# Grouped-query attention with a cached K and V: the last batches' order of work, a second buffer for turned probabilities, batch 31 placed by VectorE and ScalarE, and its V fetched in two loads

## The chip, the cores and the metric

The kernel runs on one core of one Trainium2 chip. A core has five engines that run their own instruction lists and wait for one another by semaphores: TensorE (PE, matrix products; its weight loads appear as PEld), VectorE (DVE), ScalarE (ACT), GpSimd (POOL) and SyncE (SP, which here only issues DMA transfers). The metric is the device time of one execution in microseconds, as the median of several runs; lower is better.

## The reference

For 32 batches of 4 new tokens, queries are projected, attend over a cache of 2048 keys and values in 4 KV heads (each shared by 8 of the 32 query heads), and the result is projected back:

```
B, Sq, D = 32, 4, 1024;  Hq, Hkv, Sk, Dh = 32, 4, 2048, 128
q = (x @ wq) as [B, Hq, Sq, Dh]
scores = einsum(q, k) * Dh ** -0.5          # k, v: the KV head of query head h is h // 8
p = softmax(scores)
o = einsum(p, v)                            # [B, Hq, Sq, Dh]
out = o as [B, Sq, Hq * Dh] @ wo
```

All arrays are bf16. The K and V caches are 2 MB for each batch and each of the two, 128 MB in all; wq and wo are 8 MB each.

## The kernel before

Everything is written in raw engine instructions. A small class, `Program`, keeps one ordered list of operations for each engine; an operation names the events that it waits for, and events of an engine become counts of that engine's semaphore. So **the order of the lists is the schedule**: each engine takes its own list strictly in order, and whatever stands behind a waiting operation waits too.

**Loads.** SP issues one stream: wq in 4 loads, then K and V of the batches in turn, then wo, all through a ring of 7 slots of 16 KB per partition (`slots`, `stream`, lines 145 to 186). A load waits until the operation that frees its slot is done (`freed`): the last transposition of a K (`("kt", b, 7)`) or the last quarter of a V's product (`("pv", b, 3)`). The first wo slot takes that of V of batch 26, the next that of K of 31, then V of 27, then V of 28. wo comes in ten loads (seven of 1 MB, then 512, 256 and 256 KB), each with its own semaphore.

**One batch b** passes these steps, with 128 rows = 4 KV heads x 32 (8 query heads x 4 tokens):

1. `kt_fill(b, f)`, f = 0 to 7 (PE, line 245): 8 transpositions each of K into one of three PSUM banks `ps_a`, `ps_b`, `ps_c` in turn; `evac` copies the bank to `KT_sb` (L379 on DVE, L381 on ACT; ACT takes fills 0, 1 and 7, DVE the others).
2. `qk(b, c)` (PE, line 257): the scores, 16 matmuls into `ps_s`, which holds one batch. It waits for the exponential of the batch before (`exp`), which reads `ps_s`.
3. `dve_max` (L436, L437): row maximum of the scores and its scaled negative; `act_exp` (L495): the exponential of `ps_s` into `P_sb` with the row sums. It also waits for the turn of the batch before, which reads `P_sb`.
4. `dve_turn` (L441, L442): reciprocal of the sums, and P turned in blocks of 32 x 32 from `P_sb` into `PC_sb`. `PC_sb` is one buffer: the turn waits until all four placements of the batch before have read it.
5. `place(eng, b, g)`, g = 0 to 3: rows 32g to 32g+31 of `PC_sb` go to their block of `PD_sb` (two buffers, by b modulo 2; L397 on ACT, L399 on POOL or DVE). The table `PLACE` says which engine: POOL takes three and ACT one; for batches 29 and 30 POOL takes g 0 and 1, DVE g 2, ACT g 3; for batch 31 POOL takes g 0, DVE g 1 and 2, ACT g 3.
6. `pv(b, quarter)` (PE, line 276): P times V, 16 matmuls a quarter. It waits for V's load and all four placements.
7. `dve_o` (L453) scales the product by the reciprocal sums into `o_sb`; `o_tr` (PE, line 303, called "ot" in PE's list) transposes it; `dve_ot` (L448) copies that to `oT_sb`.

At the end `oproj` (PE, line 355) multiplies `oT_sb` by wo: 64 matmuls of 512 columns in `ps_s`, in the order of the ten wo loads, two column halves for each row block. It waits for every `ot`. Then DVE (L487) copies the left half of the result and ACT (L515) the right half to `out_sb` (which is `PC_sb`), both when the last matmul is done, and SP stores it.

In the main loop (batches 0 to 28) PE's list runs the scores of batch i, the transpositions of K of i+2 and the product with V of i-2 in alternation. **The tail** is a list written out by hand. PE's list at lines 341 to 348 has: scores of 29, six fills of K of 31, the whole product of 27, scores of 30, the last two fills, ot of 27, the product of 28, scores of 31, and then the products of 29, 30 and 31, each with the ot of the batch before set in after its first quarter (for 31 after its third). DVE's list (lines 466 to 487) and ACT's (lines 507 to 515) are written to match: DVE has turn of 29, o of 27, max of 30, fill 6, ot of 27, its place of 29, o of 28, turn of 30, max of 31, ot of 28, its place of 30, o of 29, turn of 31, ot of 29, two places of 31, o and ot of 30, o and ot of 31. ACT has exp of 29, its place of 29, fill 7, exp of 30, its place of 30, exp of 31, its place of 31.

Of the kernel before, what the change touches and what calls it, by code (L numbers as in the profile page):

```python
# [5 lines left out]
ACT = mybir.ActivationFunctionType  # L6
# [49 lines left out]
def bass_standalone__gqa_block_cached__sampling_kernel(  # L56
# [28 lines left out]
    PLACE = {b: ("pool", "pool", "pool", "act") for b in range(B)}  # L85
    for b in (B - 3, B - 2):
        PLACE[b] = ("pool", "pool", "dve", "act")
    PLACE[B - 1] = ("pool", "dve", "dve", "act")
    QUARTERS = 4
    WQ_LOADS = 4  # L90
    WO_LOADS = 4
    WE = 4
# [9 lines left out]
    with ExitStack() as es:  # L102
# [3 lines left out]
        QT_sb = sb("QT_sb", [128, B, Hq, Sq], BF16)  # L106
        oT_sb = sb("oT_sb", [128, WE, WO_BLOCKS, NT], BF16)
        P_all = sb("P_sb", [128, Sk], BF16)
        PC_all = sb("PC_sb", [128, NJ // 2, 64], BF16)
        PD_sb = sb("PD_sb", [128, 2, NJ // 2, 128, 2], BF16)  # L110
        o_sb = sb("o_sb", [128, WE, Dh], BF16)
        mask = sb("mask", [128, WE], BF16)
# [4 lines left out]
        ssum = sb("ssum", [128, B], F32)  # L117
        rinv = sb("rinv", [128, B], F32)
        P_sb = P_all[:, :]
        PC_sb = PC_all[:, :, :]  # L120
        PC_flat = PC_sb.rearrange("p a b -> p (a b)")
        x_sb = P_all[:, 0:D]
        xT_sb = P_all[:, D:2 * D].rearrange("p (a b) -> p a b", b=128)
        out_sb = PC_flat[:, 0:D]

        ps_s = es.enter_context(nc.psum_tensor("ps_s", [128, Sk], F32))
        ring = [es.enter_context(nc.psum_tensor(f"ps_{c}", [128, 512], F32)) for c in "abco"]
# [12 lines left out]
        q_bank = ring_f32 + [ps_s[:, c * 512:(c + 1) * 512] for c in range(4)]  # L140

        pr.sems = {e: es.enter_context(nc.semaphore(f"s_{e}")) for e in Program.ENGINES}
        for n in ["x", "out"] + [f"slot{i}" for i in range(NSLOT)] + [f"wo{i}" for i in range(sum(map(len, WO_CUTS)))]:
            pr.sems[n] = es.enter_context(nc.semaphore(f"s_{n}"))


# [13 lines left out]
        def slot(l):  # L160
            return slots[:, slot_of[l], :]
# [4 lines left out]
        def fetch(dst, src):  # L166
            return lambda e: e.dma_start(dst, src)
# [3 lines left out]
        for n, l in enumerate(stream):  # L171
            kind, i = l
            waits = [freed(stream[n - NSLOT])] if n >= NSLOT else []
            s, v = f"slot{n % NSLOT}", 16 * (n // NSLOT + 1)
            if kind == "wq":
                pr.load("sp", fetch(slot(l), wq_v[:, i, :]), l, s, v, waits)
            elif kind in "kv":
                src = (k_cache if kind == "k" else v_cache)[i].rearrange("g (p t) d -> (g p) (t d)", t=NJ)
                pr.load("sp", fetch(slot(l), src), l, s, v, waits)
            else:  # L180
                for k in range(i * BPL, (i + 1) * BPL):
                    for e0, e1 in WO_CUTS[k]:
                        at = (k - i * BPL) * WE * D
                        part = slot(l)[:, at + e0 * D:at + e1 * D]
                        pr.load("sp", fetch(part, wo_v[k][:, e0 * D:e1 * D]), ("wo", k, e0), f"wo{n_wo}", 16, waits)
                        n_wo += 1
# [4 lines left out]
        jobs = [("kt", b, f) for b in range(B) for f in range(FILLS)]  # L191
        job_index = {j: n for n, j in enumerate(jobs)}

        def consumer(f):
            return "act" if f in ACT_FILLS else "dve"

        def ring_waits(job):
            n = job_index[job]
# [73 lines left out]
        def pv(b, quarter):  # L272
            def fn(e):
                v = slot(("v", b))
                for j in range(quarter * NJ // QUARTERS, (quarter + 1) * NJ // QUARTERS):
                    ins = e.matmul(  # L276
                        o_bank(b),
                        lhsT=PD_sb[:, b % 2, j // 2, :, j % 2],
                        rhs=v[:, j * Dh:(j + 1) * Dh],
                        start=(j == 0),  # L280
                        stop=(j == NJ - 1),
                    )
                return ins

            w = [("v", b)] + [("place", b, g) for g in range(G)]
            if b == 0:
                w += [("q_evac", 3)]
            elif b <= DRAIN - 2:
                w += [("o", b - 1), ("ot", b - 1)]
            elif b == DRAIN - 1:  # L290
                w += [("evac",) + last_in(1)]
            else:
                w += [("o", b - 2), ("ot", DRAIN - 2)]
            pr.op("pe", fn, w, ("pv", b, quarter))
# [35 lines left out]
        for i in range(DRAIN):  # L330
# [9 lines left out]
            pe_run(steps)  # L340
        pe_run([
            ("qk", B - 3, ()), ("kt", B - 1, (0, 1, 2, 3, 4, 5)),
            ("pv", B - 5, (0, 1, 2, 3)), ("qk", B - 2, ()), ("kt", B - 1, (6, 7)), ("ot", B - 5, ()),
            ("pv", B - 4, (0, 1, 2, 3)), ("qk", B - 1, ()),
            ("pv", B - 3, (0,)), ("ot", B - 4, ()), ("pv", B - 3, (1, 2, 3)),
            ("pv", B - 2, (0,)), ("ot", B - 3, ()), ("pv", B - 2, (1, 2, 3)),
            ("pv", B - 1, (0, 1, 2)), ("ot", B - 2, ()), ("pv", B - 1, (3,)), ("ot", B - 1, ()),
        ])

        def oproj(k, e0, e1):  # L350
            def fn(e):
                w = slot(("wo", k // BPL)).rearrange("p (k e n) -> p k e n", e=WE, n=D)
                for r in range(e0, e1):
                    for c in range(2):
                        ins = e.matmul(  # L355
                            ps_s[:, c * 512:(c + 1) * 512],
                            lhsT=oT_sb[:, r, k, :],
                            rhs=w[:, k % BPL, r, c * 512:(c + 1) * 512],
                            start=(k == 0 and r == 0),
                            stop=(k == WO_BLOCKS - 1 and r == WE - 1),  # L360
                        )
                return ins

            return fn

        for k in range(WO_BLOCKS):
            for e0, e1 in WO_CUTS[k]:
                pr.op("pe", oproj(k, e0, e1),
                      [("wo", k, e0)] + [("ot", b) for b in range(B)] + [("exp", B - 1)],
                      "oproj" if (k, e1) == (WO_BLOCKS - 1, WE) else None)  # L370


        def evac(b, f):
            job = ("kt", b, f)
            src = ring_bf16[job_index[job] % NRING].rearrange("p (q g r) -> p g q r", g=G, r=32)
            dst = KT_sb[:, b % 2, :, f * JPF * 32:(f + 1) * JPF * 32].rearrange("p g (q r) -> p g q r", r=32)
            w = [job] + ([("qk", b - 2, 3)] if b >= 2 else [])
            if consumer(f) == "dve":
                pr.op("dve", lambda e: e.tensor_copy(dst, src), w, ("evac",) + job)  # L379
            else:  # L380
                pr.op("act", lambda e: e.activation(dst, src, ACT.Copy), w, ("evac",) + job)  # L381
# [8 lines left out]

        def place(eng, b, g):
            rows = slice(32 * g, 32 * (g + 1))
            src = PC_sb[rows, :, :]
            dst = PD_sb[rows, b % 2, :, 32 * g:32 * (g + 1), :].rearrange("p a h e -> p a (h e)")
            w = [("ptr", b), ("zero", 1)] + ([("pv", b - 2, QUARTERS - 1)] if b >= 2 else [])
            if eng == "act":
                pr.op("act", lambda e: e.activation(dst, src, ACT.Copy), w, ("place", b, g))  # L397
            else:
                pr.op(eng, lambda e: e.tensor_copy(dst, src), w, ("place", b, g))  # L399
# [15 lines left out]

        def dve_fills(b, fs):
            for f in fs:
                if b is not None and consumer(f) == "dve":
                    evac(b, f)

        def act_fills(b, fs):
            for f in fs:
                if b is not None and consumer(f) == "act":
                    evac(b, f)

        grid = ident[:, :].rearrange("p (a h s) -> p a h s", h=WE, s=Sq)
# [12 lines left out]

        def dve_turn(i):  # L440
            pr.op("dve", lambda e: e.reciprocal(rinv[:, i:i + 1], ssum[:, i:i + 1]), [("exp", i)], ("rinv", i))  # L441
            pr.op("dve", lambda e: e.transpose(PC_flat.bitcast(U32), P_sb.bitcast(U32)),  # L442
                  [("exp", i)] + [("place", i - 1, g) for g in range(G) if i > 0], ("ptr", i))

        def dve_ot(b):
            dst = oT_sb[:, :, :, b * Sq:(b + 1) * Sq]
            src = oT_bank(b).rearrange("p (e h s) -> p e h s", e=WE, s=Sq)
            pr.op("dve", lambda e: e.tensor_copy(dst, src), [("otr", b)], ("ot", b))  # L448
# [17 lines left out]
        dve_max(B - 3)  # L466
        dve_fills(B - 1, range(0, 6))
        dve_turn(B - 3)
        dve_o(B - 5)
        dve_max(B - 2)  # L470
        dve_fills(B - 1, range(6, FILLS))
        dve_ot(B - 5)
        places("dve", B - 3)
        dve_o(B - 4)
        dve_turn(B - 2)
        dve_max(B - 1)
        dve_ot(B - 4)
        places("dve", B - 2)
        dve_o(B - 3)
        dve_turn(B - 1)  # L480
        dve_ot(B - 3)
# [2 lines left out]
        dve_ot(B - 2)  # L484
        dve_o(B - 1)
        dve_ot(B - 1)
        pr.op("dve", lambda e: e.tensor_copy(out_sb[:, 0:512], ps_s[:, 0:512]), ["oproj"], "out0")  # L487


        for j in range(1, NB, 2):  # L490
# [15 lines left out]
            act_fills(i + AHEAD, range(5, FILLS))  # L506
        act_fills(B - 1, range(0, 5))
        act_exp(B - 3)
        places("act", B - 3)
        act_fills(B - 1, range(5, FILLS))  # L510
        act_exp(B - 2)
        places("act", B - 2)
        act_exp(B - 1)
        places("act", B - 1)
        pr.op("act", lambda e: e.activation(out_sb[:, 512:1024], ps_s[:, 512:1024], ACT.Copy), ["oproj"], "out1")  # L515

        block = es.enter_context(nc.Block())

# [49 lines left out]
```

## Time and profile before

| | us |
|---|---|
| time, median of 3 runs (lowest, highest) | 371.54 (371.36, 371.87) |
| time of the profiled execution | 371.67 |
| its span, first to last instruction | 369.9 |
| PE busy / PEld busy | 315.0 / 274.1 |
| DVE busy / ACT busy / POOL busy | 254.2 / 240.1 / 187.8 |
| DMA, mean over the span | 412 GB/s |

Times in the trace are microseconds from the first instruction. A row of the timeline gives the start, the length, the engine, the source line, the operation, the output and inputs, the shapes and how many instructions were merged; in brackets stands the idle time before it and what ended it. PE's instructions are pipelined, so that the next one starts before the one before has left the array. A view of a source line gives, for the transfers that it issued, the time from issue to landing.

### The profile page before, as it was taken

Reading aid. Unit: us, or ns where it says so; the run is one execution under the profiler, and the core shown is the slowest. Engines: PE = TensorE matmul, PEld = TensorE weight load, DVE = VectorE, ACT = ScalarE, POOL = GpSimd, SP = SyncE. Lnnn points to the kernel's source line nnn. Section 1 sums busy time; section 2 is a strip of 40 time slices with the busy share of each in tenths; the row PEclk is TensorE's granted clock in tenths of the full one; section 3 lists DMA queues with packets and bytes.
Section 4 is the critical chain, followed back from the end, with each engine's and each line's share of the span. In section 5 each row is a group of like instructions: output and inputs, shape, how many; then the busy total and the mean of one; then the engine's idle time right before and its main releaser. Section 6 shows DMA issues by size and latency. Waiting matters only on the chain.

```text
span 369.9 us, 11029 instructions
## 1 busy us (share of the span) xinstructions
PE 315.0 (85%) x5062; PEld 274.1 (74%) x5064; DVE 254.2 (69%) x364; ACT 240.1 (65%) x198; POOL 187.8 (51%) x100
## 2 busy tenths in 40 slices
PE   0997877999988888878889988799888869998886
PEld 0896657888887777767778887697777759886742
DVE  0025877888877777768877777488777785989600
ACT  1016678888877777776777777577777774877200
POOL 9600066666655556666555555366666663654200
PEclk9999989999999999999999999899999998999999
DMA  8999999999999999999999999999999999999972
GB/s 321 443 423 423 427 423 423 430 425 423 425 426 425 425 423 427 434 425 423 421 429 423 425 427 425 427 427 425 423 425 423 431 430 425 423 423 420 417 314 81
DMA packets 11567, 152.24 MB, mean 412 GB/s; under 512 B 1280, under 2 KB 1280, under 8 KB 1920
## 3 DMA queue, kind: packets, MB, share of 16 engines
q1 hardware_dynamic: 11376, 151.26, 96.7%
q8 instruction: 40, 0.66, 0.7%
q10 hardware_dynamic: 144, 0.26, 0.2%
q14 instruction: 7, 0.06, 0.0%
HBM read 151.26 MB, written 0.26 MB: 410 GB/s over the span
## 4 chain that ended last, share of the span: by engine, by line
DMA 52%; PE 26%; ACT 12%; DVE 7%; issue 1%; SPq 0%
DMA slots<-in_v_cache_dram 45%; PE ps_o L276 12%; DMA slots<-in_k_cache_dram 7%; ACT KT_sb L381 5%; PE ps_s L355 4%; ACT P_sb L495 4%; ACT PD_sb L397 3%; PE ps_a L245 3%; PE ps_c L245 3%; DVE PC_sb L442 2%; PE ps_b L245 2%; DVE mx L436 2%; DVE PD_sb L399 1%; PE ps_s L257 1%; PE ps_b L276 1%
## 5 line engine op out<-in xcount | busy, mean ns | idle before, releaser
L399 POOL COPY PD_sb<-PC_sb 32x2048 bf16<-32x2048 bf16 x92 | 173.4, 1885 | 157.1 <-DVE PC_sb L442 142.8
L276 PE MATMUL ps_o<-slots,PD_sb 128*128 128x128 bf16 x1920 | 119.4, 221 | 29.4 <-DMA slots<-in_v_cache_dram 28.1
L276 PEld LDWEIGHTS ps_o<-slots,PD_sb 128*128 128x128 bf16 x1920 | 111.1, 99 | 33.6 <-DMA slots<-in_v_cache_dram 31.7
L397 ACT ACTIVATE PD_sb<-PC_sb 32x2048 bf16<-32x2048 bf16 x32 | 61.0, 1907 | 72.4 <-DVE PC_sb L442 64.8
L495 ACT ACTIVATE P_sb<-ps_s,negmx 128x2048 bf16<-128x2048 f32 x32 | 81.8, 2558 | 1.7 <-DVE negmx L437 0.9
L436 DVE TENSOR_REDUCE mx<-ps_s 128x1 f32<-128x2048 f32 x32 | 73.2, 2289 | 4.2 <-PE ps_s L257 3.9
L245 PE MATMUL ps_a<-ident,slots 128*128 128x128 bf16 x688 | 53.3, 221 | 3.4 <-DMA slots<-in_k_cache_dram 1.2
L245 PE MATMUL ps_c<-ident,slots 128*128 128x128 bf16 x680 | 53.0, 222 | 3.1 <-ACT KT_sb L381 2.1
L245 PE MATMUL ps_b<-ident,slots 128*128 128x128 bf16 x680 | 53.0, 222 | 1.9 <-ACT KT_sb L381 1.7
L379 DVE COPY KT_sb<-ps_c 128x1024 bf16<-128x1024 bf16 x54 | 36.8, 681 | 22.8 <-PE ps_c L245 22.8
L379 DVE COPY KT_sb<-ps_b 128x1024 bf16<-128x1024 bf16 x53 | 36.1, 682 | 19.3 <-PE ps_b L245 19.1
L245 PEld LDWEIGHTS ps_a<-ident,slots 128*128 128x128 bf16 x688 | 41.5, 99 | 9.7 <-issue 5.2
L245 PEld LDWEIGHTS ps_c<-ident,slots 128*128 128x128 bf16 x680 | 41.4, 99 | 9.7 <-issue 5.0
L379 DVE COPY KT_sb<-ps_a 128x1024 bf16<-128x1024 bf16 x53 | 36.1, 681 | 17.7 <-PE ps_a L245 17.7
L245 PEld LDWEIGHTS ps_b<-ident,slots 128*128 128x128 bf16 x680 | 41.2, 99 | 8.0 <-issue 4.2
L442 DVE STREAM_TRANSPOSE PC_sb<-P_sb 128x1024 uint32<-128x1024 uint32 x32 | 39.2, 1225 | 0.0
L381 ACT ACTIVATE KT_sb<-ps_a 128x1024 bf16<-128x1024 bf16 x33 | 33.8, 1025 | 3.5 <-PE ps_a L245 3.3
L381 ACT ACTIVATE KT_sb<-ps_b 128x1024 bf16<-128x1024 bf16 x32 | 32.8, 1024 | 2.9 <-PE ps_b L245 2.6
L257 PE MATMUL ps_s<-KT_sb,QT_sb 128*32 128x512 bf16 x512 | 33.5, 382 | 0.7 <-ACT P_sb L495 0.7
L381 ACT ACTIVATE KT_sb<-ps_c 128x1024 bf16<-128x1024 bf16 x31 | 31.7, 1024 | 0.2
L453 DVE SCALAR_TENSOR_TENSOR o_sb<-ps_o,rinv,mask 128x512 bf16<-128x512 f32 x30 | 21.4, 713 | 1.6 <-PE ps_o L276 1.6
L257 PEld LDWEIGHTS ps_s<-KT_sb,QT_sb 128*32 128x32 bf16 x512 | 10.7, 96 | 9.1 <-ACT P_sb L495 1.1
(46 smaller groups left out, 146.1 us busy)
## 6 DMA issues: line engine op xcount, KB each, us to landing
slots<-in_k_cache_dram SPq DMA_DIRECT2D x32, 2048.0 KB, 27.9
slots<-in_v_cache_dram SPq DMA_DIRECT2D x32, 2048.0 KB, 23.4
slots<-in_wq_dram SPq DMA_DIRECT2D x4, 2048.0 KB, 14.6
slots<-in_wo_dram SPq DMA_DIRECT2D x7, 1024.0 KB, 25.4
slots<-in_wo_dram SPq DMA_DIRECT2D x1, 512.0 KB, 26.9
slots<-in_wo_dram SPq DMA_DIRECT2D x2, 256.0 KB, 23.2
P_sb<-in_x_dram ACTq DMA_DIRECT2D x1, 256.0 KB, 8.1
out_dram<-PC_sb SPq DMA_DIRECT2D x1, 256.0 KB, 2.0
```

The source lines that it names most:

```text
L245: ins = e.transpose(dst[:, q * 128:(q + 1) * 128], slot(("k", b))[:, j * Dh:(j + 1) * Dh], ident[:, :],)
L257: ins = e.matmul(ps_s[32 * g:32 * (g + 1), c * 512:(c + 1) * 512], lhsT=QT_sb[:, i, REP * g:REP * (g + 1), :], rhs=KT_sb[:, i % 2, g, c * ...
L276: ins = e.matmul(o_bank(b), lhsT=PD_sb[:, b % 2, j // 2, :, j % 2], rhs=v[:, j * Dh:(j + 1) * Dh], start=(j == 0), stop=(j == NJ - 1),)
L355: ins = e.matmul(ps_s[:, c * 512:(c + 1) * 512], lhsT=oT_sb[:, r, k, :], rhs=w[:, k % BPL, r, c * 512:(c + 1) * 512], start=(k == 0 and r ...
L379: pr.op("dve", lambda e: e.tensor_copy(dst, src), w, ("evac",) + job)
L381: pr.op("act", lambda e: e.activation(dst, src, ACT.Copy), w, ("evac",) + job)
L397: pr.op("act", lambda e: e.activation(dst, src, ACT.Copy), w, ("place", b, g))
L399: pr.op(eng, lambda e: e.tensor_copy(dst, src), w, ("place", b, g))
L436: pr.op("dve", lambda e: e.tensor_reduce(mx[:, i:i + 1], ps_s[:, :], AX.X, ALU.max), [("qk", i, 3)], ("max", i))
L442: pr.op("dve", lambda e: e.transpose(PC_flat.bitcast(U32), P_sb.bitcast(U32)), [("exp", i)] + [("place", i - 1, g) for g in range(G) if i ...
L453: pr.op("dve", lambda e: e.scalar_tensor_tensor(out=o_sb[:, :, :], in0=src, scalar=rinv[:, b:b + 1], in1=keep, op0=ALU.mult, op1=ALU.mult) ...
L495: pr.op("act", lambda e: e.activation(P_sb.rearrange("p (a r e) -> p a e r", r=32, e=2), ps_s[:, :].rearrange("p (a e r) -> p a e r", r=32 ...
```

## The change

The main loop keeps its lists but for one wait. In the tail:

- `PC_sb` gets a second buffer, chosen by b modulo 2; the turn of batch i now waits for the placements of i-2 instead of i-1. This holds in the main loop too.
- PE's hand-written list: the scores of 30 stand between the two halves of the product of 27, whose second half and the last two fills follow; ot of 27 stands after the first quarter of the product of 28, the scores of 31 before its last quarter; ot of 28 stands after three quarters of the product of 29, ot of 29 and ot of 30 after two quarters of the products of 30 and 31.
- DVE evacuates the last fill (K of 31, f = 7) in place of ACT.
- DVE's list: max of 30 before o of 27; turn of 30 and max of 31 before o of 28; its place of 30 before ot of 28.
- ACT's list: exp of 30 before its place of 29.
- Batch 31: POOL places nothing, DVE three of the four blocks, ACT one as before.
- V of 31 comes in two loads of 1 MB, one for each half of every partition's row, the second with a semaphore of its own, for which the last two quarters of its product wait.
- The last two matmuls of `oproj` are two operations with an event each, so that DVE's copy of the left half waits only for the first.

```diff
-    PLACE[B - 1] = ("pool", "dve", "dve", "act")
+    PLACE[B - 1] = ("dve", "dve", "dve", "act")
...
-        PC_all = sb("PC_sb", [128, NJ // 2, 64], BF16)
+        PC_all = sb("PC_sb", [128, 2, NJ // 2, 64], BF16)
...
-        PC_sb = PC_all[:, :, :]
-        PC_flat = PC_sb.rearrange("p a b -> p (a b)")
+        PC_sb = [PC_all[:, z] for z in range(2)]
+        PC_flat = [pc.rearrange("p a b -> p (a b)") for pc in PC_sb]
...
+                if l == ("v", B - 1):
+                    half = SLOT // 2
+                    pr.load("sp", fetch(slot(l)[:, 0:half], src[:, 0:half]), l, s, v, waits)
+                    pr.load("sp", fetch(slot(l)[:, half:], src[:, half:]), ("v2", i), "v2", 16, waits)
+                else:
+                    pr.load("sp", fetch(slot(l), src), l, s, v, waits)
...
-        def consumer(f):
-            return "act" if f in ACT_FILLS else "dve"
+        def consumer(b, f):
+            return "act" if f in ACT_FILLS and (b, f) != (B - 1, FILLS - 1) else "dve"
...
             w = [("v", b)] + [("place", b, g) for g in range(G)]
+            if b == B - 1 and quarter >= QUARTERS // 2:
+                w.append(("v2", b))
...
-            ("pv", B - 5, (0, 1, 2, 3)), ("qk", B - 2, ()), ("kt", B - 1, (6, 7)), ("ot", B - 5, ()),
-            ("pv", B - 4, (0, 1, 2, 3)), ("qk", B - 1, ()),
-            ("pv", B - 3, (0,)), ("ot", B - 4, ()), ("pv", B - 3, (1, 2, 3)),
-            ("pv", B - 2, (0,)), ("ot", B - 3, ()), ("pv", B - 2, (1, 2, 3)),
-            ("pv", B - 1, (0, 1, 2)), ("ot", B - 2, ()), ("pv", B - 1, (3,)), ("ot", B - 1, ()),
+            ("pv", B - 5, (0, 1)), ("qk", B - 2, ()), ("pv", B - 5, (2, 3)), ("kt", B - 1, (6, 7)),
+            ("pv", B - 4, (0,)), ("ot", B - 5, ()), ("pv", B - 4, (1, 2)), ("qk", B - 1, ()), ("pv", B - 4, (3,)),
+            ("pv", B - 3, (0, 1, 2)), ("ot", B - 4, ()), ("pv", B - 3, (3,)),
+            ("pv", B - 2, (0, 1)), ("ot", B - 3, ()), ("pv", B - 2, (2, 3)),
+            ("pv", B - 1, (0, 1)), ("ot", B - 2, ()), ("pv", B - 1, (2, 3)), ("ot", B - 1, ()),
...
-        def oproj(k, e0, e1):
+        def oproj(k, e0, e1, cs):
...
-                    for c in range(2):
+                    for c in cs:
...
-                pr.op("pe", oproj(k, e0, e1),
-                      [("wo", k, e0)] + [("ot", b) for b in range(B)] + [("exp", B - 1)],
-                      "oproj" if (k, e1) == (WO_BLOCKS - 1, WE) else None)
+                last = (k, e1) == (WO_BLOCKS - 1, WE)
+                for cs in ((0,), (1,)) if last else ((0, 1),):
+                    pr.op("pe", oproj(k, e0, e1, cs),
+                          [("wo", k, e0)] + [("ot", b) for b in range(B)] + [("exp", B - 1)],
+                          ("oproj", cs[0]) if last else None)
...
-            src = PC_sb[rows, :, :]
+            src = PC_sb[b % 2][rows, :, :]
...
-            pr.op("dve", lambda e: e.transpose(PC_flat.bitcast(U32), P_sb.bitcast(U32)),
-                  [("exp", i)] + [("place", i - 1, g) for g in range(G) if i > 0], ("ptr", i))
+            pr.op("dve", lambda e: e.transpose(PC_flat[i % 2].bitcast(U32), P_sb.bitcast(U32)),
+                  [("exp", i)] + [("place", i - 2, g) for g in range(G) if i > 1], ("ptr", i))
...
         dve_turn(B - 3)
+        dve_max(B - 2)
         dve_o(B - 5)
-        dve_max(B - 2)
         dve_fills(B - 1, range(6, FILLS))
         dve_ot(B - 5)
         places("dve", B - 3)
-        dve_o(B - 4)
         dve_turn(B - 2)
         dve_max(B - 1)
+        dve_o(B - 4)
+        places("dve", B - 2)
         dve_ot(B - 4)
-        places("dve", B - 2)
         dve_o(B - 3)
...
-        pr.op("dve", lambda e: e.tensor_copy(out_sb[:, 0:512], ps_s[:, 0:512]), ["oproj"], "out0")
+        pr.op("dve", lambda e: e.tensor_copy(out_sb[:, 0:512], ps_s[:, 0:512]), [("oproj", 0)], "out0")
...
         act_exp(B - 3)
+        act_exp(B - 2)
         places("act", B - 3)
-        act_fills(B - 1, range(5, FILLS))
-        act_exp(B - 2)
         places("act", B - 2)
         act_exp(B - 1)
         places("act", B - 1)
-        pr.op("act", lambda e: e.activation(out_sb[:, 512:1024], ps_s[:, 512:1024], ACT.Copy), ["oproj"], "out1")
+        pr.op("act", lambda e: e.activation(out_sb[:, 512:1024], ps_s[:, 512:1024], ACT.Copy), [("oproj", 1)], "out1")
```

## The prediction

> **What bounds the kernel now.** First the page's slices and the shares of the chain of waits.
>
> ```profile
> DMA  8999999999999999999999999999999999999972
> DMA 52%; PE 26%; ACT 12%; DVE 7%; issue 1%; SPq 0%
> ```
>
> The DMA engines are full until the last two slices, so only the tail can change. How far it can shrink depends on when wo is there: the issues in line 167's view, first a 1 MB load (wo's block 6), then the last load.
>
> ```profile
> L167 SPq DMA_DIRECT2D slots<-in_wo_dram x1: 327/327/327, 335.4 to 335.4; - x1
> DMA to landing us min/median/max: 26.0/26.0/26.0
> ...
> L167 SPq DMA_DIRECT2D slots<-in_wo_dram x1: 1770/1770/1770, 342.3 to 342.3; - x1
> DMA to landing us min/median/max: 21.6/21.6/21.6
> ```
>
> Block 6 lands at 335.4 + 26.0 = 361.4, the last piece at 342.3 + 21.6 = 363.9. Then PE's timeline at the end:
>
> ```profile
> 342.04 1.05 PE L276 MATMUL ps_b<-slots,PD_sb 128*128 128x128 bf16 x16 [1.33 <-DVE PD_sb L399]
> ...
> 347.24 2.84 PE L276 MATMUL ps_o<-slots,PD_sb 128*128 128x128 bf16 x48 [1.34 <-DVE PD_sb L399]
> ...
> 352.94 13.76 PE L355 MATMUL ps_s<-slots,oT_sb 128*128 128x512 bf16 x62 [0.69 <-DVE oT_sb L448]
> ```
>
> The 64 matmuls of the output run without a gap, 13.76 / 64 = 0.215 each, to 366.70. wo bounds them 16 matmuls from the end: 361.4 + 16 x 0.215 = 364.85. **So the tail before them can save 1.85 at most.** It waits for DVE's places, for which DVE, POOL and ACT are read together:
>
> ```profile
> 334.00 0.68 DVE L399 COPY PD_sb<-PC_sb 32x2048 bf16<-32x2048 bf16 x1
> 339.94 1.84 DVE L399 COPY PD_sb<-PC_sb 32x2048 bf16<-32x2048 bf16 x1
> 343.98 3.00 DVE L399 COPY PD_sb<-PC_sb 32x2048 bf16<-32x2048 bf16 x2
> ...
> 329.80 3.83 POOL L399 COPY PD_sb<-PC_sb 32x2048 bf16<-32x2048 bf16 x2 [3.82 <-PE ps_o L276]
> 337.40 3.83 POOL L399 COPY PD_sb<-PC_sb 32x2048 bf16<-32x2048 bf16 x2 [3.78 <-DVE PC_sb L442]
> 343.83 1.88 POOL L399 COPY PD_sb<-PC_sb 32x2048 bf16<-32x2048 bf16 x1 [2.60 <-DVE PC_sb L442]
> ...
> 343.81 1.91 ACT L397 ACTIVATE PD_sb<-PC_sb 32x2048 bf16<-32x2048 bf16 x1 [1.49 <-DVE PC_sb L442]
> ```
>
> A DVE place takes 0.68 alone. Beside POOL's it ends 0.55 after POOL: 341.78 after 341.23, and (the chain splits the pair into 2.28 and 0.69) 346.26 after 345.71. DVE stands still meanwhile, with everything behind it.
>
> **The change, step by step**, from the last common point, the product of 27 at 325.93. Earlier nothing moves: the turn (L442) has 0.0 idle before it on the page, so the main loop never waited for the single buffer. Durations: half a product 1.79, a quarter 0.89, scores 0.98 (1.05 to the result), a fill 0.45, ot 0.13, max to negative 2.33, exponential to reciprocal 2.64, turn 1.15 (1.23 to the result), o 0.66 (0.75), DVE to product 0.26 (346.98 to 347.24).
>
> *Scores of 30.* Exponential 29 ends at 327.60; after half the product of 27 PE is free at 325.93 + 1.79 = 327.72 (before: 329.59), and the second half ends 330.49, the last two fills 331.39. Max of 30 follows the turn of 29 at 328.86 (before 330.69), exponential 30 starts 331.37 (before 333.20) and releases `ps_s` at 334.0. Gain so far 1.83.
>
> *Behind max of 30* now stand o of 27 (331.26), fills 6 (331.93) and 7 (332.53, ACT's work moved here, 0.60) and ot of 27 (333.13), then DVE's place of 29 at 333.44. POOL's two places of 29 wait for the whole product of 27 (330.64): 330.77 to 334.60. So the place that was free before (334.00, 0.68) now waits for POOL, and ends 334.60 + 0.55 = 335.15. The turn of 30, whose sums are ready at 334.01, starts with its reciprocal at 335.18, before 336.05. **The gain falls to 0.87.** ACT's place of 29, now behind exponential 30, ends 334.0 + 1.91 = 335.9; PE reaches the product of 29 at 336.07, so this move costs nothing, with 0.1 to spare. The second `PC_sb` lets the turn of 30 not wait for that; with one it would lose 0.7.
>
> *Scores of 31* start after three quarters of the product of 28, at 331.39 + 0.89 + 0.13 + 1.79 = 334.20, so max of 31 waits for DVE alone: 335.25 + 1.15 = 336.40. Exponential 31 starts 338.88 (before 339.74), its sums are there at 341.52. DVE goes on with o of 28 at 338.77, and its place of 30 at 339.55; POOL places 30 from 336.53 to 340.36, so DVE ends at 340.91 (before 341.78). Product of 30: 341.17 (before 342.04). ot of 28 and o of 29 follow, reciprocal of 31 341.91, turn 341.98 to 343.21 (before 342.55 to 343.77): gain 0.57.
>
> *Batch 31.* ot of 29 is later in PE's list: 341.17 + 1.79 + 0.28 = 343.24, DVE copies it 343.27 to 343.53. Then three places without POOL. A place followed by another instruction held it up until its own end (346.26, next 346.30; 346.98, next 347.01), so each costs 0.72: ends 344.24, 344.96, 345.67. ACT's ends 343.24 + 1.91 = 345.15. Before: 346.98. Removed are 2.28 + 0.03 + 0.69 = 3.00, added 2.12. **Gain 1.31.** The unknown is a DVE place beside ACT's: at least 0.68; at most as if ACT held DVE up as POOL does. I take 0.69, because the place begun at 339.94 ran on for 2 us after ACT's had ended (339.28) and stopped by POOL's end.
>
> By the Trainium skill (SBUF — State Buffer, Who interferes with whom) the port pair that is locked is VectorE's and GpSimd's, and ScalarE has its own. The blocked row at 343.98 can't tell the two, as both ended near 345.71; by that page the sum stands at 1.40, by the other reading it is 0.
>
> *Product of 31 to the end.* PE starts it at 345.93, ends two halves with an ot between at 349.64 (before 350.93), and the way to the output, 2.01 before (350.93 to 352.94), has the same o, ot and copy: 351.63. 64 matmuls end at 365.39; block 6 is needed at 351.63 + 48 x 0.215 = 361.95, after 361.4, the last piece at 364.96, after 363.9: no wait. Half a result's copy: DVE's 0.69 now starts 0.215 before the last matmul, ACT's 0.60 ends last: 0.09 gained.
>
> *V of 31 in two loads* gains nothing: its product waits until 345.93 for the places, and V's single load lands at 320.9 + 23.1 = 344.0. The price: one more issue on SP (0.43) ahead of ten issues of wo, the last finishing at 344.0 for a landing at 363.9; a delay as long as a whole further load (2.45) still leaves wo queued behind others. In size two halves cost what one load does: six wo loads of 1 MB land from 321.3 + 25.4 = 346.7 to 361.4, 2.45 each, a 2 MB V takes 4.9 (313.0 + 26.2 = 339.2 to 344.0). Bounds: 0, and 0.1 for two short gaps. wo's slots are freed at 331.5 (K of 31, as before) and 336.2 (V of 28, 0.9 later), some 20 us ahead.
>
> A rule speaks against it: the Trainium skill (DMA: Bandwidth & Descriptors, Anatomy of one DMA) gives each DMA about 2.0 us fixed. If that were serial, wo's end would go to 365.9 and the gain shrink to about 0.4; the 2.45 rows show loads in a queue hiding it.
>
> **Sum**: 1.31 + 0.09 = 1.40. The profiled 371.67 becomes 370.27; it stands 0.13 above the median, so 371.54 - 1.40 = **370.1**.
>
> **Rivals.** (1) *ACT's place holds DVE's up*: for it, the row at 343.98; against it, 339.94. The first place of 31 then ends 345.15 + 0.55 = 345.70, the third 347.13, against 346.98: gain gone, 371.6. (2) *DVE's places are slow by themselves* when three run in a row beside ACT: at 1.84 each, from 343.56, they end 349.15, 2.17 late, less 0.09: **373.6, slower**. It decides from (346.98 - 343.56) / 3 = 1.14 each. Against it: 0.68 and 0.69 whenever POOL was still. (3) *wo binds*: the chain gains more than 1.85 (POOL's place of 29 not in DVE's way would give up to 0.95 more), time 371.54 - 1.94 = 369.6; or wo lands up to 1.4 late and most of the gain is lost. (4) *The split or the new order does not reach the end*: a tail that is bound elsewhere, 371.5.
>
> **How the numbers follow.** Forecast (369.6 to 370.8) 0.64; rival 3 at its floor 0.06; rivals 1 and 4 and a late wo 0.14; rival 2 and others that lose 0.16. 0.2% is 0.74 us, what a measurement of this kernel can tell from no change. Faster: 0.64 + 0.06 = 0.70; within: 0.14; slower: 0.16. The range reaches from the floor, less 0.1 for the spread of runs, 369.5, to the case of no gain, 371.6; that leaves out 0.16.
>
> **What will show it.** Scores of 30 some 1.87 before those of today, relative to the product of 27; DVE's place of 29 near 1.7 long, ending 0.55 after POOL; three places of 0.69 in a row; no gap in the output's matmuls; PE's wait ahead of the product of 31 still put down to DVE's place. Wrong if a place beside ACT is over 1.1, if ACT's place of 29 becomes what the product of 29 waits for, or if the matmuls of the output wait for wo.

## The result, and the profile after

| | before | changed |
|---|---|---|
| time, median (lowest, highest), 6 runs each | 371.64 (371.36, 371.87) | 370.10 (370.06, 370.18) |
| profiled execution / its span | 371.67 / 369.9 | 370.08 / 368.3 |
| product of 27 starts | 325.93 | 325.48 |
| places of 31 end | 346.98 | 345.24 |
| product of 31 starts | 347.24 | 345.35 |
| last matmul of the output ends | 366.70 | 365.13 |

The ratio is 0.9959, with a 95% interval of 0.9947 to 0.9972: 1.5 us faster, where 1.4 was forecast. Part of it came by other steps than the forecast had.

The page's slices and the shares of the chain of waits in the changed kernel:

```profile
DMA  8999999999999999999999999999999999999983
DMA 66%; PE 21%; ACT 9%; DVE 2%; issue 1%; SPq 0%
```

DVE was 7% of the chain and is 2%, DMA went from 52% to 66%; 7 of the 66 are loads of wo. Why can be read in the end of that chain, in order of time (start, length, what):

```profile
336.00 25.45 DMA slots<-in_wo_dram
361.45 0.05 issue
361.50 0.61 PE ps_s L362 x2
362.11 0.05 issue
362.16 2.98 PE ps_s L362 x13
365.14 0.02 issue
365.16 0.60 ACT PC_sb L523
```

Before, the chain came through DVE's places into the output's product and never met wo. Now its last link is a transfer: wo's block 6, issued at 336.00 and landed at 361.45, and behind it the last 16 matmuls (one record is missing). The same end in PE's timeline:

```profile
345.35 1.95 PE L281 MATMUL ps_o<-slots,PD_sb 128*128 128x128 bf16 x32 [0.65 <-DVE PD_sb L408]
...
351.05 14.08 PE L362 MATMUL ps_s<-slots,oT_sb 128*128 128x512 bf16 x62 [0.69 <-DVE oT_sb L457]
```

Two of the 64 records are missing here and in the kernel before, in both one of them the first: the idle time ahead is 0.69, and 0.48 in profiles that have all 64. So the products truly start 0.21 earlier, at 350.84 and 352.73. Before, it took 13.97, the length of this row wherever all 64 records are there and PE waits for nothing; now 14.29, so 0.32 of what the tail gained is spent waiting for wo. The places in DVE's timeline:

```profile
333.02 1.78 DVE L408 COPY PD_sb<-PC_sb 32x2048 bf16<-32x2048 bf16 x1
334.83 0.16 DVE L450 RECIPROCAL rinv<-ssum 128x1 f32<-128x1 f32 x1
...
339.19 1.38 DVE L408 COPY PD_sb<-PC_sb 32x2048 bf16<-32x2048 bf16 x1
...
343.14 2.10 DVE L408 COPY PD_sb<-PC_sb 32x2048 bf16<-32x2048 bf16 x3
```

and POOL's and ACT's beside them:

```profile
330.43 3.83 POOL L408 COPY PD_sb<-PC_sb 32x2048 bf16<-32x2048 bf16 x2 [4.90 <-PE ps_o L281]
336.20 3.83 POOL L408 COPY PD_sb<-PC_sb 32x2048 bf16<-32x2048 bf16 x2 [1.95 <-DVE PC_sb L451]
```
```profile
342.93 1.91 ACT L406 ACTIVATE PD_sb<-PC_sb 32x2048 bf16<-32x2048 bf16 x1 [1.78 <-DVE PC_sb L451]
```

The first two of DVE's end 0.54 and 0.54 after POOL's pairs (334.80 after 334.26, 340.57 after 340.03). The three of 31 take 0.70 each, the first two of them wholly beside ACT's.

The profiles also differ ahead of the tail. Windows of 2 us (length; busy time and instructions of PE, PEld, DVE, ACT, POOL; TensorE's granted clock; DMA share, GB/s), first of the kernel before, then of the changed one:

```profile
306.00:308.00 2.00, 2.00 (x25) 2.00 (x22) 0.00 (x0) 0.00 (x0) 0.00 (x0) 0.56 0.94 393
308.00:310.00 2.00, 2.00 (x25) 2.00 (x23) 1.56 (x4) 0.00 (x0) 0.00 (x0) 0.59 1.10 467
```
```profile
306.00:308.00 2.00, 2.00 (x40) 2.00 (x38) 0.59 (x1) 0.00 (x0) 0.00 (x0) 1.00 0.92 385
308.00:310.00 2.00, 2.00 (x40) 2.00 (x38) 2.00 (x5) 0.06 (x1) 0.03 (x1) 1.00 1.06 451
```

The profiled execution of before had its clock halved for 3.4 us there (0.44 and 0.41 of the clock are missing in 2 us each, which at half the clock makes 3.4 us); the changed one's had not. The change is not the reason: of what runs there only the turn's wait differs, and two kernels below that are the kernel before in all that runs until then were not halved there either. With this goes most of the 0.45 by which the product of 27 starts earlier (all twelve profiles are compared below). Set against that start, the chain to the output's product went from 26.80 (352.73 - 325.93) to 25.36 (350.84 - 325.48): **the change is worth 1.44 in the chain**, and the rest is this difference of one execution.

### The profile page after: what moved, and what is told of

Its sections match the earlier page's. It is cut to its first block, busy times and chain, and to the rows that moved or that the text cites. A ratio compares the mean times of both kernels' runs of the same rounds, so it can differ in the third digit from the quotient of the medians.

```text
span 368.3 us, 11026 instructions
## 1 busy us (share of the span) xinstructions
PE 312.9 (85%) x5062; PEld 271.5 (74%) x5064; DVE 254.3 (69%) x366; ACT 239.1 (65%) x197; POOL 186.0 (50%) x99
## 4 chain that ended last, share of the span: by engine, by line
DMA 66%; PE 21%; ACT 9%; DVE 2%; issue 1%; SPq 0%
DMA slots<-in_v_cache_dram 52%; PE ps_o L281 10%; DMA slots<-in_k_cache_dram 7%; DMA slots<-in_wo_dram 7%; ACT KT_sb L390 5%; PE ps_a L250 3%; PE ps_b L250 3%; ACT P_sb L504 2%; ACT PD_sb L406 2%; PE ps_c L250 2%; DVE PC_sb L451 1%; PE ps_s L262 1%; PE ps_b L281 1%; PE ps_s L362 1%; DVE mx L445 1%
## 5 line engine op out<-in xcount | busy, mean ns | idle before, releaser
L408 POOL COPY PD_sb<-PC_sb 32x2048 bf16<-32x2048 bf16 x91 | 171.5, 1885 | 153.3 <-DVE PC_sb L451 144.9
L250 PE MATMUL ps_b<-ident,slots 128*128 128x128 bf16 x680 | 52.1, 219 | 2.1 <-ACT KT_sb L390 2.0
L250 PEld LDWEIGHTS ps_b<-ident,slots 128*128 128x128 bf16 x680 | 40.4, 98 | 8.2 <-issue 4.2
L390 ACT ACTIVATE KT_sb<-ps_a 128x1024 bf16<-128x1024 bf16 x32 | 32.8, 1025 | 3.5 <-PE ps_a L250 3.3
```

Source lines behind the costliest of these rows:

```text
L250: ins = e.transpose(dst[:, q * 128:(q + 1) * 128], slot(("k", b))[:, j * Dh:(j + 1) * Dh], ident[:, :],)
```

## The experiments

The theory: the places of batch 31 and the order around the scores of 30 and 31 set the start of the output's product, and 0.3 behind that lies wo's arrival. Rivals: the chain alone sets the end; wo alone does; or one part of the change brings it all. Each kernel was timed beside the kernel before on the same chip, which had medians of 371.55 (22 runs), 371.68 (15) and 371.80 (11) in the three sets. The changed kernel was not timed again in them, so some 0.2 of a difference from its 370.10 can come from the set alone; the ratio to the kernel before and the rows of the profile are safer.

**All but the placement of 31.** The changed kernel with

```diff
-    PLACE[B - 1] = ("dve", "dve", "dve", "act")
+    PLACE[B - 1] = ("pool", "dve", "dve", "act")
```

> The changed kernel, with batch 31 placed as before (POOL one block, DVE two, ACT one). Theory: DVE's first place of 31 waits for POOL's again and ends some 0.5 us after it; POOL's would run from about 342.9 to 344.8, so the places end near 346.1 instead of 345.24, the output's product starts near 351.9 instead of 351.05; since the changed kernel already loses some 0.3 there in waiting for wo, the time rises by only 0.5, to 370.6. Rival (DVE is not held up by POOL, or this part is hidden): no change, 370.1. Rival (nothing but this chain counts, wo plays no part): 0.85 more, 370.95.

Measured: 371.13 (370.46 to 371.35), ratio to before 0.999 [0.9981, 0.9999]. DVE's and POOL's rows:

```profile
343.53 2.84 DVE L408 COPY PD_sb<-PC_sb 32x2048 bf16<-32x2048 bf16 x2
```
```profile
343.23 1.89 POOL L408 COPY PD_sb<-PC_sb 32x2048 bf16<-32x2048 bf16 x1 [2.93 <-PE ps_c L310]
```

DVE is held up as expected, its first place lasting until 0.54 after POOL's end at 345.12. The loss is 1.03, twice what the theory said and more than its rival. Its mechanism stands, its size was wrong twice: from the last place to PE's next product it takes 0.26 again instead of 0.11 (346.37 to 346.63; see below), and this profile has the halved clock near 305, after which the changed kernel has hardly any time at wo to lose. Against the product of 27, the product of 31 starts 1.02 later than in the changed kernel. All the other edits together are worth 0.42.

**The placement of 31 alone.** The kernel before with the line above turned round.

> The kernel before, with the placement of batch 31 by DVE (three blocks) and ACT (one) as its only edit. Theory: the places of 31 begin at 343.98 as before and take 3 x 0.70 = 2.1 instead of 3.0, so 0.9 less in the chain, and wo (which binds from 1.85 less) is not reached: 370.75. If the orders of PE, DVE and ACT were what brought the gain: within 0.2 of the kernel before, 371.6.

Measured: 370.33 (370.15 to 370.57), ratio 0.997 [0.9959, 0.9982], 1.22 less. One line of the diff thus brings four fifths of the gain. Expected was 0.9. Against the start of the product of 27, the product of 31 starts 20.14 later instead of 21.31, 1.17 less: 0.10 ahead of the places (17.95 instead of 18.05), 0.91 in them, as this row shows (2.09 instead of 3.00),

```profile
343.39 2.09 DVE L399 COPY PD_sb<-PC_sb 32x2048 bf16<-32x2048 bf16 x3
```

and 0.16 behind them, which the theory had left out: PE starts the product of 31 at 345.58, 0.10 after their end at 345.48. This profile is one without the halved clock, and there the output's row of 64 takes 14.03 instead of 13.97: wo is just reached, which the expectation had excluded.

**One buffer for turned P.** The changed kernel with

```diff
-        PC_sb = [PC_all[:, z] for z in range(2)]
+        PC_sb = [PC_all[:, 0] for z in range(2)]
...
-                  [("exp", i)] + [("place", i - 2, g) for g in range(G) if i > 1], ("ptr", i))
+                  [("exp", i)] + [("place", i - 1, g) for g in range(G) if i > 0], ("ptr", i))
```

> The changed kernel with one buffer for turned P, and the turn of a batch waiting for the places of the batch before, as in the kernel before. Theory: the turn of 30 waits for ACT's place of 29, which stands behind exponential 30 and ends at 335.5, so it starts near 335.55 instead of 334.91; all of the chain moves by 0.6 to 0.65, and with the 0.3 that is lost to wo anyway the time rises by 0.3, to 370.4. Rival (the buffer is not what the turn waits for): 370.1. Without any slack at wo: 370.75.

Measured: 370.74 (370.41 to 371.05), ratio 0.9979 [0.9971, 0.9988]; 0.64 more than the changed kernel. The wait is where it was expected, on DVE:

```profile
335.87 1.25 DVE L451 STREAM_TRANSPOSE PC_sb<-P_sb 128x1024 uint32<-128x1024 uint32 x1 [0.55 <-ACT PD_sb L406]
```

Against the product of 27 the turn is 0.65 later (10.08 instead of 9.43). So exponential 30 can be ahead of ACT's place of 29 at no cost only because the second buffer is there. The time rose by the whole 0.65 and not by half. In this profile, which has the halved clock, there is no wait for wo to be filled; that the spare 0.3 is missing in most executions is concluded from the median.

**V of 31 in one load.** The changed kernel with `if l == ("v", B - 1):` and the test for the second semaphore made false.

> The changed kernel with V of 31 in one load. Theory: V is there by 344.1 and its product starts at 345.35, so the split buys nothing; without it wo may land up to 0.1 earlier, since it landed at 361.45 and 364.00 instead of 361.37 and 363.90: 370.0 to 370.1. Rival (the split is part of the gain): 370.5 or more.

Measured: 370.10 (369.87 to 370.25), ratio 0.9965 [0.9953, 0.9978]: the same as with two. The split neither gains nor costs anything that these runs can tell. V lands at 344.19 and its product starts at 345.23.

**wo's first block left out, after and before.** In each kernel

```diff
-                for k in range(i * BPL, (i + 1) * BPL):
+                for k in range(max(1, i * BPL), (i + 1) * BPL):
...
-                            rhs=w[:, k % BPL, r, c * 512:(c + 1) * 512],
+                            rhs=w[:, max(1, k) % BPL, r, c * 512:(c + 1) * 512],
...
-                          [("wo", k, e0)] + [("ot", b) for b in range(B)] + [("exp", B - 1)],
+                          [("wo", max(1, k), e0)] + [("ot", b) for b in range(B)] + [("exp", B - 1)],
```

> The changed kernel without the load of wo's first block of 1 MB: the output's product uses the rows of the second block in its place, with as many matmuls. The DMA stream ends 2.45 us earlier, all else is as it was. Theory (wo's arrival binds the last 16 matmuls): the product of the output runs through, 13.76 instead of 14.08, so 0.1 to 0.35 less: 369.75 to 370.0. Rival (the chain alone): 370.1. Rival (the DMA stream sets the end throughout): 2.4 less, 367.7.

> The kernel before without the load of wo's first block (the second block's rows are used in its place). Theory: there the product of the output starts 1.85 too late for wo to matter, so no change, 371.6. Rival (the DMA stream binds there too): up to 2.4 less, 369.2.

Measured: after, 370.08 (369.61 to 370.31), ratio 0.9956 [0.9944, 0.9969]; before, 371.53 (371.10 to 372.24), ratio 0.9998 [0.9989, 1.0007]. The kernel before doesn't care about wo, as expected. The changed kernel's median fell short of the 0.1 to 0.35: it did not move. But its spread did, from 0.12 to 0.70, and its fastest run is 0.45 faster than any of the changed kernel. In its profile, which has the halved clock, the product of 27 starts at 325.91, the output's product at 351.29, and the 64 matmuls run through in 13.97 to 365.26, within 0.13 of where wo would have held them anyway:

```profile
351.29 13.97 PE L362 MATMUL ps_s<-slots,oT_sb 128*128 128x512 bf16 x64 [0.47 <-DVE oT_sb L457]
```

So, it seems, **wo cuts off what the faster executions would have had, and the slower ones just meet it**. The clock that each run was granted on average supports it: it is 0.995 in the four profiles without the halved clock near 305 and 0.980 to 0.991 in the eight with it. Of the kernel before, 10 of the 48 runs had 0.994 or more and took 371.02 to 371.43, median 371.17; the other 38 have a median of 371.70. Without wo's first block, too, the fastest run (369.61) is the one with the highest clock, 0.995. In the changed kernel the clock makes no difference: 370.08 to 370.18 at 0.995, 370.06 at 0.985. The spread alone would be a weak argument: the changed kernel's six runs lie within 0.12, but those of V in one load and of the shorter chain below, which wo holds up in the same way, spread by 0.38 and 0.35.

**A shorter chain.** The changed kernel with

```diff
-    for b in (B - 3, B - 2):
-        PLACE[b] = ("pool", "pool", "dve", "act")
+    PLACE[B - 2] = ("dve", "dve", "dve", "act")
...
         places("dve", B - 2)
+        dve_turn(B - 1)
         dve_ot(B - 4)
         dve_o(B - 3)
-        dve_turn(B - 1)
-        dve_ot(B - 3)
         places("dve", B - 1)
+        dve_ot(B - 3)
```

> The changed kernel with a shorter chain ahead of the output: POOL places three blocks of 29 and none of 30, DVE three of 30 (so that none of DVE's places runs beside POOL's), and DVE's turn of 31 stands ahead of ot of 28 and o of 29, its places of 31 ahead of ot of 29. By the rows the turn of 30 starts about 1.1 earlier, the places of 31 end about 0.6 earlier, and the product of the output starts near 350.5. Theory (wo binds): the end stays, 370.0 to 370.1, and the product of the output is 0.6 longer. Rival (the chain alone): 369.5.

Measured: 370.13 (370.01 to 370.36), ratio 0.9959 [0.9947, 0.9972]. The chain is shorter: the output's product starts 24.92 after the product of 27 (350.80 - 325.88) instead of 25.36, though by 0.44, not 0.6. And PE's timeline shows where that went:

```profile
350.80 10.52 PE L361 MATMUL ps_s<-slots,oT_sb 128*128 128x512 bf16 x48 [0.48 <-DVE oT_sb L456]
361.71 3.63 PE L361 MATMUL ps_s<-slots,oT_sb 128*128 128x512 bf16 x16 [0.39 <-DMA slots<-in_wo_dram]
```

The first 48 matmuls run through, then PE stands 0.39 for block 6.

**Block 6 in two loads, alone and with the shorter chain.**

```diff
-    WO_CUTS = [[(0, WE)]] * (WO_BLOCKS - 1) + [[(0, 2), (2, 3), (3, 4)]]
+    WO_CUTS = [[(0, WE)]] * (WO_BLOCKS - 2) + [[(0, 2), (2, 4)], [(0, 2), (2, 3), (3, 4)]]
```

> The changed kernel with wo's block 6 in two loads of 512 KB and nothing else. Theory: the chain and wo stand so near each other that one alone gives little: where TensorE's clock dropped near 305 us the output's product starts some 0.4 later and meets no wait, so nothing is gained; where it did not, 0.3. Median 369.8 to 370.1, with more spread than the changed kernel's 0.12. Rival (wo's landing is the one limit): 369.65, as with the shorter chain. Rival (the cut costs): over 370.2.

> The same shorter chain, and wo's block 6 in two loads of 512 KB, so that PE can begin it when half is there (near 360.2 instead of 361.45). Theory: the last stretch that wo binds is then the pieces of block 7 (362.7, 363.4, 364.0), the last matmul ends near 364.5 instead of 365.14: 369.5. Rival (more, smaller loads cost what they save, or the chain binds): 370.1. If only the chain binds: 369.5 without the cut too.

Measured: alone 369.95 (369.71 to 370.29), ratio 0.9955 [0.9941, 0.9969]; with the shorter chain **369.66 (369.45 to 369.71), ratio 0.9946 [0.9933, 0.9958]**, the fastest kernel of this study, and each of its runs is below each of the changed kernel's. PE's row there:

```profile
350.74 13.97 PE L361 MATMUL ps_s<-slots,oT_sb 128*128 128x512 bf16 x64 [0.48 <-DVE oT_sb L456]
```

No gap is left. The shorter chain alone gives nothing (370.13), the cut alone 0.15 by the medians, with intervals that overlap widely, both together 0.44. The shorter chain with and without the cut was timed on the same chip, and all five runs with it are below all five without. Two limits stand within half a microsecond of each other, and each hides what is done to the other.

**An event of POOL more.** The changed kernel, in which POOL clears 4 columns of a spare tile after its last place, and the product of 31 waits for that too:

```diff
             places("pool", b)
+        pr.op("pool", lambda e: e.memset(spare[:], 0.0), [("place", B - 2, 1)], "tick")
...
-            w = [("v", b)] + [("place", b, g) for g in range(G)]
+            w = [("v", b)] + ["tick"] * (b == B - 1) + [("place", b, g) for g in range(G)]
```

> The changed kernel with one more event: after its last place POOL clears a spare tile of 4 columns, and the product of 31 waits for that too, although it is done some 5 us before. Theory A (the time from the last place's end to the first matmul, 0.25 where POOL is among the placers and 0.11 where it is not, goes with the number of engines that PE's wait names): 0.25 at the product of 31, time 370.1 to 370.25. Theory B (it goes with POOL's copies themselves): 0.11 as in the changed kernel, 370.1.

Measured: 370.34 (370.20 to 370.46), ratio 0.9963 [0.9949, 0.9978]. The rows of PE, and of DVE behind its last place:

```profile
345.94 1.95 PE L282 MATMUL ps_o<-slots,PD_sb 128*128 128x128 bf16 x32 [0.81 <-DVE PD_sb L409]
```
```profile
343.58 2.10 DVE L409 COPY PD_sb<-PC_sb 32x2048 bf16<-32x2048 bf16 x3
```

The places end at 343.58 + 2.10 = 345.68, the matmuls start 0.26 later, as where POOL is one of the placers, although POOL had long been done. Theory A holds: it goes with the wait for a third engine, not with POOL's copies. The time, 370.34, is above what either theory said and doesn't decide; the rows do. One rival is left, that it goes with POOL as such, and the shorter chain answers it: there POOL and ACT alone place batch 29, and POOL ends last, at 330.83 + 5.77 = 336.60.

```profile
330.83 5.77 POOL L407 COPY PD_sb<-PC_sb 32x2048 bf16<-32x2048 bf16 x3 [4.90 <-PE ps_o L280]
```
```profile
336.71 2.84 PE L280 MATMUL ps_o<-slots,PD_sb 128*128 128x128 bf16 x48 [0.33 <-issue]
```

PE starts 0.11 later, as with two engines. A third engine other than POOL was not tried.

## Why the prediction was right, and where not

*What bounds it.* DMA full to the end and the places in the chain are seen, and wo's floor too, but nearer. It was set at block 6's landing plus 16 x 0.215 = 3.44; measured are 3.68 (361.45 to 365.13), and 3.67 in the profiles of one load of V (361.50 to 365.17) and of the shorter chain (361.66 to 365.33). So the tail could save 366.70 - 365.13 = 1.57 and not 1.85. The 0.215 came from a row of 62 records divided by 64, and is right by luck: rows of 16, 48 and 64 matmuls take 3.63, 10.52 and 13.97, which is 0.215 for each matmul and some 0.2 at the end of the row. Left out were these 0.2, which the missing first record hid, and the 0.05 from the landing to the first matmul.

*The orders: 0.57 forecast at the turn of 31.* Measured against the start of the product of 27: 16.62 before (342.55), 16.19 after (341.67), so 0.43. The step that was off was the half product ahead of the scores of 30, taken as 1.79: PE started the scores 1.88 after it (325.48 to 327.36):

```profile
325.48 1.95 PE L281 MATMUL ps_o<-slots,PD_sb 128*128 128x128 bf16 x32
327.36 1.05 PE L262 MATMUL ps_s<-KT_sb,QT_sb 128*32 128x512 bf16 x16
```

The profile before shows it as well: there the scores start 3.66 after the whole product (325.93 to 329.59), not 2 x 1.79. POOL, which waits for the second half, started its places of 29 later by 0.11 than forecast, and DVE's place of 29 ended later by 0.10. The lock at that place was right: its 1.78, and its end 0.54 after POOL's. The shorter chain, in which that place is POOL's, turns 30 at 8.22 after the product of 27 (334.10 - 325.88) instead of 9.43.

*The places of 31: 2.12 in place of 3.00.* Measured 2.10. Rivals 1 and 2 fall by the same row, 343.14 to 345.24, at 0.70 a place beside ACT's (342.93 to 344.84). The page of the Trainium skill that gives ScalarE its own ports (SBUF — State Buffer, Who interferes with whom) is borne out by it.

*PE's start behind them* was costed at 0.26 and measured 0.11, a gain of 0.15 that the sum did not have. What the turn fell short of came back at ot of 29, which did not hold up the first place, so the places start 0.39 earlier (17.66 after the product of 27 instead of 18.05; forecast 0.42). The chain's 1.44 is 0.39 + 0.90 in the places + 0.15; 1.31 was forecast, so that without the 0.15 it would have been 1.29.

*The end* was forecast without a wait for wo, and there it failed: "block 6 is needed at ... 361.95, after 361.4 ... no wait". That the output's matmuls wait for wo is one of the prediction's own signs of being wrong, and it came, with 0.32. The tail was anchored at 325.93, one execution's start of the product of 27, behind a halved clock. Where the clock was not halved near 305, the start is 325.34 to 325.48 (four of the twelve profiles here, of whatever kernel), else 325.74 to 326.00 (the other eight). From the early starts the changed chain runs into block 6, so that rival 3 holds there; from the late ones its 1.44 leads just up to that floor. So the exact hit of 370.1 owes something to luck: the sum lacked a gain of 0.15 and, in some executions, a wait of 0.3, and the medians hide this. Against the runs of the kernel before with a clock of 0.994 or more (median 371.17) only some 1.1 is gained, against the others (371.70) 1.6.

*V in two loads* gains nothing, as forecast, and costs nothing: its halves land 2.49 apart (341.63 and 344.12). The fixed cost of about 2.0 by the Trainium skill (DMA: Bandwidth & Descriptors, Anatomy of one DMA) is measured there for transfers that GpSimd issues. Those here are issued by SP, and in their filled queue no such cost adds up: one load or two, the last piece of wo lands at 364.04 or 364.00.

*The copy of the left half* ended before ACT's, as forecast, but the store is issued at 365.85, 0.72 after the last matmul, instead of 0.75: 0.09 was forecast, 0.03 came.

## What to carry to other kernels

Look for one instruction with two lengths in the trace, and at what ends just before the long one: here three copies on one engine beat a fair share between two engines that lock each other out. Before shortening a chain, compute the floor of the transfers behind it with the landing times of the trace, from more than one execution: a limit 0.3 us away makes half a microsecond of work invisible, until both are moved together. A fall in the spread of the runs can be a hint that another limit has taken over, but compare it run by run with the granted clock before you believe it.

## What was not expected of the hardware

From the end of the last place to PE's first matmul behind it: 0.10 to 0.11 where PE waits for two engines (DVE and ACT, or POOL and ACT), 0.25 to 0.26 where POOL is a third beside DVE and ACT, even when it was done 4.6 us before.

TensorE's clock was halved for 3.4 us near 305 in eight of the twelve profiles and not in the other four, after PE had stood still for 2.80 (before, halved) or 2.76 us (after, not) in waiting for V; that V was one load behind one that took 6.5 us instead of 4.9. The kernel before was halved, and two kernels that are the same up to there (the placement of 31 alone, and wo's first block left out of the kernel before) were not. The length of the idle time alone does not decide: 2.40 to 2.80 us in the halved profiles, 2.35 to 2.76 in the others. What does stays open; no run here tried it. The start of the product of 27 goes with it by about 0.4 us in all twelve profiles; that it is what spreads the times of the kernel before is argued from this and from the clocks of the runs, not shown.
